# DVE, ACT and POOL choose their next operation by a due time that is found backward from TensorE's order, over rounds of planning

## The chip, the cores and the metric

The kernel runs on one core of a Trainium2 chip. The metric is the device time of one execution in microseconds (us), as a median over runs. One further execution is profiled, and every row below is from that one. The engines are called PE (TensorE matmul), PEld (TensorE weight load), DVE (VectorE), ACT (ScalarE), POOL (GpSimd) and SP, which issues nearly all DMAs.

## The reference

Random-feature attention for 8 batches of 8 heads (576 positions, head size 64, 128 features), then a gated MLP on the 4608 rows that come out of it (512 to 1536 and back).

```python
q_s, k_s = q * scale, k * scale
phi(x) = exp(h - max(h)) / sqrt(m),  h = x @ omega.T - sum(x*x)/2
kv  = einsum('bhsm,bhsd->bhmd', phi(k_s), v);  z = sum over s of phi(k_s)
num = einsum('bhsm,bhmd->bhsd', phi(q_s), kv)
den = einsum('bhsm,bhm->bhs', phi(q_s), z) + 1e-6
x   = (num / den) laid out as [4608, 512]
out = ((x @ w_a) * (x @ w_b)) @ w_out
```

## The kernel before

**Work.** Attention goes pair by pair of heads (32 pairs, four to a batch). The MLP goes in nine blocks of 512 rows: blocks 0 to 7 are the first 512 positions of each batch, block 8 is the last 64 positions of all eight batches. While the MLP of one batch runs, attention of the next fills in. fp32 operands of the MLP are split into a high and a low part (`hilo`, `split`, `convert`), and each product is three matmuls. Blocks 0 and 1 multiply plainly (`moe_block`, L1074) while ACT and DVE still convert the weights; blocks 2 to 8 use seven half-size products where eight would do plainly (`moe_block7`, `product`, L1165), and blocks 7 and 8 do so for the output projection too (`Out7`, L971; otherwise L903).

**What hangs on what.** In `moe_block7` the products of a unit share two PSUM tiles p0 and p1. After each pair DVE adds them into a tile c (L1175), and only then may PE write p0 or p1 again. At the end of two units DVE multiplies two c tiles (L1214), ACT or DVE casts the result to the high part of `ghl`, DVE subtracts for the low part (L283), and the output products read `ghl`. Outputs of blocks 0 to 6 are copied from PSUM to `osb` by ACT or DVE and stored by SP; `osb` has two places, raw0 and raw1, so a copy waits until the store from its place has landed. Block 8 gets its rows from DRAM: a DMA brings `xl`, ACT casts it to `x` (one cast for each quarter, x_0 to x_3).
The pair work has a burst on PE (L696 with L764 and L766): it needs `kl` and `hq`, which come back transposed by way of DRAM, and writes pkv and pm.

**Order.** Nothing here is in program order: the kernel first records a graph of 5661 operations, each with engines that may do it, a cost, and a priority number `prio` written by hand (adds into c -12, casts to ghl -10, output sums -7 to -9, weight conversion 4000 to 8000, attention 1000 times the pair, PE's MLP products 10**6 upward). `Graph.schedule` plans them one after another on modelled engines and rings of tiles, and the kernel issues each engine's instructions in the planned order. Among the operations that could start on an engine, the one with the lowest key is planned next:

```python
wait = CFG["WAIT"] if e == "DVE" and 0 <= o.prio < 4000 else 0
key = (max(s - wait, free[e] + 30), o.prio, o.n)
```

At run time each engine goes through its own list in that order, and each instruction waits for its semaphores. What the model has wrong turns into waits. An operation that lists two engines (casts to ghl, copies to osb, casts of weights) goes to the one that the plan finds earlier.

Of the kernel before, what the change touches and what calls it, by code (L numbers as in the profile page):

```python
# [35 lines left out]
EPS = 1e-6 * M  # L36
KS = NHP

CFG = dict(ZS=800, ZB=(1500, 3000, 5000), ZD=(1500, 3000, 4500), HQ=(2500, 4000, 5000), BACK2=(1500, 2500, 4000), TW=(), WAIT=150, RAW=2000, FAST=(0, 1, 2, 3), JOIN0=False, WARM=8, HROOM=["w0", "u1", "w1", "u2", "w2", "u3"], H=3, TURN=(7,), BACK=1500, AT=2, GATES=(-4, -1, 2, 5), SQPE=4, MARGIN=1200, LOAD=2500, SUMS=1000, NATS=(1, 2, 3), CONV=(28000, 2600))

# [8 lines left out]


class Op:
    __slots__ = ("eng", "fn", "deps", "prio", "alloc", "margin", "n", "end", "start", "after", "bytes", "need", "at")


class Graph:
# [15 lines left out]
    def op(self, eng, fn, r=(), w=(), prio=0, alloc=(), deps=(), margin=0, nbytes=0, at=0):  # L73

        o = Op()
        o.eng, o.fn, o.prio, o.alloc, o.margin, o.bytes = eng, fn, prio, list(alloc), margin, nbytes
        o.n, o.end, o.start, o.at = len(self.ops), None, None, at
        found = set(deps)
        for b in o.alloc:
            b.born = o  # L80
        found.update(b.born for b, _ in (*r, *w) if b.born is not None)
        for b, part in r:
            found.update(x for x, p in b.writers if p is None or part is None or p == part)
        for b, part in w:
            found.update(x for x, p in b.writers + b.readers if p is None or part is None or p == part)
        for b, part in w:
            keep = lambda l: [(x, p) for x, p in l if not (part is None or p == part)]
            b.writers, b.readers = keep(b.writers) + [(o, part)], keep(b.readers)
            b.users.append(o)
        for b, part in r:  # L90
            b.readers.append((o, part))
            b.users.append(o)
        for b in o.alloc:
            if b.ring in self.rings:
                self.rings[b.ring]["order"].append(b)
        found.discard(o)
        o.deps = list(found)
        self.ops.append(o)
        return o
# [13 lines left out]
    def place(self, o):  # L113
# [16 lines left out]
            got.append((b, best[1]))  # L130
        return t, got

    def schedule(self, bw=330.0, dma_lat=2000):
        engines = ("PE", "ACT", "DVE", "POOL", "SP")
        free = dict.fromkeys(engines, 0)
        dma_free = 0
# [20 lines left out]
        while len(done) < len(self.ops):  # L157
            best = None
            for e in engines:
                mine = None  # L160
                for o in ready[e]:
                    at = self.place(o) if o.alloc else (0, ())
                    if at is None:
                        continue
                    s = max(free[e], o.need, at[0])
                    for x in o.eng:
                        if x != e and max(free[x], o.need, at[0]) + o.eng[x] <= s + o.eng[e] - (o.eng[e] <= o.eng[x]):
                            break
                    else:


                        wait = CFG["WAIT"] if e == "DVE" and 0 <= o.prio < 4000 else 0
                        key = (max(s - wait, free[e] + 30), o.prio, o.n)
                        if mine is None or key < mine[0]:
                            mine = key, s, o, at[1]
                if mine and (best is None or mine[1] < best[1]):
                    best = (*mine, e)
# [57 lines left out]
def tile_attention_moe(ctx: ExitStack, tc: tile.TileContext, kqt, kqtt, kqn, kqnt, vx, omst, idn, wab, wout, out):  # L235
# [1045 lines left out]

    order = g.schedule()
    with tc.manual_schedule():
        for o in order:
            for b in o.alloc:
# [70 lines left out]
```

## Time and profile before

| what | value |
|---|---|
| median of 3 runs | 1063.78 us (1063.69 to 1069.8) |
| the profiled execution | 1066.55 us, its span 1064.7 us |
| mean granted TensorE clock | 0.998 |
| busy share: DVE, ACT, POOL | 84%, 56%, 10% |
| DMA | 314.16 MB, mean 295 GB/s |

The span is the time from the first to the last instruction; 1.85 us of the profiled execution lie around it. The profiled execution is 2.77 us above the median. A matmul's recorded end is modelled and overlaps the next matmul, so what PE loses at a place is best read from start to start.

### The profile page before, as it was taken

What the parts mean: (1) busy time and instruction counts of PE and PEld (TensorE: products, weight loads), DVE (VectorE), ACT (ScalarE), POOL (GpSimd) and SP (SyncE); (2) the same over time, 40 slices, a digit from 0 to 9 for tenths busy, and PEclk for the clock granted to TensorE, in tenths of its full rate; (3) what the DMA queues carried; (4) which work ended last, traced back from release to release, by engine and by line L of the source; (5) the groups of instructions that cost most, each with busy time, mean ns of one, the idle gap of its engine ahead of it and who ended that gap; (6) DMA issues with size and microseconds to landing.
All of it is one profiled execution on the core that took longest, in us unless ns stands there. A gap on an engine that the chain in (4) does not pass through costs nothing.

```text
span 1064.7 us, 22028 instructions
## 1 busy us (share of the span) xinstructions
PE 1045.8 (98%) x7806; PEld 920.4 (86%) x7806; DVE 892.0 (84%) x2233; ACT 599.1 (56%) x1646; POOL 107.5 (10%) x177
## 2 busy tenths in 40 slices
PE   9999999999989999999999999999999999999997
PEld 7877777777779888888888888888889988999997
DVE  6999998899997788778878889778777768998766
ACT  7999787667575574657455665666563233233211
POOL 0111111111111010111011111111010000000000
PEclk9999999999999999999999999999999999999999
DMA  9867878999899889999899888988888798899981
GB/s 357 304 228 243 278 260 282 300 345 311 284 309 359 275 285 302 335 312 289 308 328 311 299 303 296 336 293 272 270 294 275 257 336 286 306 335 342 349 304 45
DMA packets 123614, 314.16 MB, mean 295 GB/s; under 512 B 17648, under 2 KB 40944, under 8 KB 123504
## 3 DMA queue, kind: packets, MB, share of 16 engines
q1 hardware_dynamic: 122640, 312.10, 86.3%
q8 instruction: 61, 1.00, 0.4%
q10 hardware_dynamic: 864, 0.66, 0.2%
q14 instruction: 49, 0.40, 0.1%
HBM read 255.52 MB, written 57.18 MB: 294 GB/s over the span
## 4 chain that ended last, share of the span: by engine, by line
PE 77%; DVE 13%; DMA 4%; ACT 3%; issue 2%; SPq 0%; ACTq 0%; DVEq 0%
PE p L1165 37%; PE o L903 18%; PE ppk L454 5%; PE o_P L971 4%; PE pa L1074 3%; PE pb L1074 2%; PE pkv L696 2%; PE pm L764 2%; DVE zero L715 1%; DVE c L1175 1%; DVE sm L477 1%; DMA td<-ts 1%; DMA out_dram<-osb 1%; PE pn L838 1%; DVE ghl L283 1%
## 5 line engine op out<-in xcount | busy, mean ns | idle before, releaser
L1175 DVE TENSOR_TENSOR c<-p,c 128x512 f32<-128x512 f32 (+1 forms) x336 | 207.9, 619 | 92.5 <-PE p L1165 89.9
L903 PE MATMUL o<-wo,ghl 128*128 128x512 f32 x1008 | 270.1, 397 | 0.8 <-DVE ghl L283 0.8
L903 PEld LDWEIGHTS o<-wo,ghl 128*128 128x128 f32 x1008 | 176.1, 188 | 33.4 <-DVE ghl L283 1.6
L1165 PE MATMUL p<-Sa,t 128*128 128x256 f32 x1008 | 141.4, 281 | 0.0
L1165 PEld LDWEIGHTS p<-Sa,t 128*128 128x128 f32 x1008 | 131.0, 188 | 4.4
L649 POOL TENSOR_TENSOR z<-hk 128x256 f32<-128x256 f32 x56 | 43.9, 783 | 660.3 <-ACT hk L490 559.5
L275 ACT COPY c<-p 128x256 f32<-128x256 f32 x84 | 31.1, 370 | 120.3 <-PE p L1165 66.8
L725 ACT ACTIVATE hq<-hq,dn 128x128 f32<-128x128 f32 x224 | 71.0, 393 | 39.4 <-DVE dn L721 39.4
L454 PEld LDWEIGHTS ppk<-om,X 64*128 64x128 f32 x504 | 61.8, 189 | 18.3 <-issue 5.2
L715 DVE CUSTOM_DVE_ANT_0 zero<-hq,zb 128x128 bf16<-128x128 f32 x224 | 75.0, 335 | 2.9 <-ACT c L275 0.2
L454 PE MATMUL ppk<-om,X 64*128 64x128 f32 x504 | 74.6, 288 | 2.3 <-ACT k L275 2.1
L1165 PE MATMUL p<-x,t 128*128 128x256 f32 x504 | 74.4, 284 | 0.8 <-ACT oc L275 0.8
L1165 PE MATMUL p<-Sb,t 128*128 128x256 f32 x504 | 74.6, 284 | 0.0
L1074 PE MATMUL pa<-x,wa 128*128 128x512 f32 x288 | 73.8, 399 | 0.5 <-ACT a L275 0.5
L1074 PE MATMUL pb<-x,wb 128*128 128x512 f32 x288 | 73.0, 398 | 1.2 <-ACT xts L275 0.6
L1165 PEld LDWEIGHTS p<-x,t 128*128 128x128 f32 x504 | 69.3, 190 | 5.5 <-ACT oc L275 1.0
L454 PE MATMUL ppq<-om,X 64*128 64x128 f32 x504 | 73.0, 286 | 0.6 <-ACT hq L275 0.3
L1165 PE MATMUL p<-Sb,bq 128*128 128x256 f32 x504 | 73.6, 282 | 0.0
L1165 PE MATMUL p<-x,wb 128*128 128x256 f32 x504 | 70.1, 283 | 2.5 <-DVE c L1175 2.4
L490 ACT ACTIVATE hk<-hk,sm 128x128 f32<-128x128 f32 x184 | 59.3, 393 | 23.0 <-DVE sm L485 22.9
L1165 PEld LDWEIGHTS p<-x,wb 128*128 128x128 f32 x504 | 65.7, 188 | 6.2 <-DVE c L1175 3.1
L1165 PE MATMUL p<-x,wa 128*128 128x256 f32 x504 | 69.9, 284 | 1.0 <-DVE c L1175 1.0
(192 smaller groups left out, 2025.6 us busy)
## 6 DMA issues: line engine op xcount, KB each, us to landing
t<-td SPq DMA_DIRECT2D x168, 512.0 KB
wo<-wod SPq DMA_DIRECT2D x96, 512.0 KB
bq<-bd SPq DMA_DIRECT2D x84, 256.0 KB
qdr<-qd SPq DMA_DIRECT2D x112, 160.0 KB
hq<-qdr SPq DMA_DIRECT2D x28, 640.0 KB
X<-in_kqt_dram SPq DMA_DIRECT2D x30, 512.0 KB
raw<-in_wab_dram SPq DMA_DIRECT2D x24, 512.0 KB
td<-ts SPq DMA_DIRECT2D x24, 512.0 KB
```

The costliest lines, as they stand in the source:

```text
L275: nc.scalar.copy(o(), i())
L454: nc.tensor.matmul(pps[w].ap[:, c * M:c * M + M], x()[rows, c * P:c * P + P], om.ap[rows], start=True, stop=True)
L490: g.op({"ACT": 392}, lambda e, c=c, w=w, to=to, at=at: nc.scalar.activation(to.ap[:, at + c], src[w](c), AF.Exp, scale=SC, bias=sm.ap[:, 2 ...
L649: g.op({"POOL": pool2(n)}, lambda e: nc.gpsimd.tensor_tensor(o(), a(), c(), op=ALU.add), r=r, w=w, alloc=list(al), prio=pri, deps=zload[-1 ...
L696: nc.tensor.matmul(pkv.ap[D * j:D * j + D, 0:M], vb.ap[:, vc, 0:D], c(), start=(n == 0), stop=(n == 4))
L715: g.op({"DVE": 413}, lambda e, c=c, j=j, rr=rr, qc=qc: nc.vector.tensor_tensor_reduce(out=junk.ap[rr], in0=qc(), in1=zb.ap[rr, j], scale=1 ...
L725: g.op({"ACT": 392}, lambda e, c=c, src=src: nc.scalar.activation(hq.ap[:, c], src(), AF.Copy, scale=dn.ap[:, c:c + 1]), r=[sd, (dn, None) ...
L903: nc.tensor.matmul(po.ap[:], ghl.ap[:, gi, t * P:(t + 1) * P], wo.ap[:, wi], start=(n == 0 and i == 0), stop=(n == NF - 1 and i == 2))
L971: nc.tensor.matmul(pb.ap[:, t], A[0](ai)[:, t * P:(t + 1) * P], W[0](wi), start=begin and t == j == 0, stop=stop and t == 1 and j == 2)
L1074: nc.tensor.matmul(pb.ap[:], wt.ap[:, wi, c], xs[c].at(xi), start=(c == 0 and i == 0), stop=(c == NC4 - 1 and i == 2))
L1165: nc.tensor.matmul(pb.ap[:, half], wcol(wi, c), xc(xi, c), start=n == 0, stop=n == 5)
L1175: g.op({"DVE": dve(n)}, lambda e: nc.vector.tensor_tensor(c4.ap[:, o], pb.ap[:, half], y(), op=ALU.add), r=[*((pb, k) for k in range(half. ...
```

## The change

`Graph.plan` takes the place of the one call of `schedule`. It plans once as before. Then, three times, `dues` goes backward through the last plan: each PE operation is due when that plan had it, less all idle time of PE up to it, and every other operation is due at the least of its users' due times less their cost and latency; the next plan uses the due time instead of `prio` among DVE's, ACT's and POOL's candidates. PE and SP still choose by `prio`. Of the four plans the one with the earliest planned end is issued. No operation is added or taken out and no cost is changed; the graph has the same dependencies.

```diff
-CFG = dict(ZS=800, ...
+CFG = dict(EDF=("DVE", "ACT", "POOL"), ROUNDS=3, SQUEEZE=1, ZS=800, ...
...
+    def dues(self):
...
+        last = {}
+        for o in self.order:
+            for b in o.alloc:
+                if b.slot in last:
+                    for x in last[b.slot].users:
+                        if x is not o:
+                            after[x].append(o)
+                last[b.slot] = b
+        idle, at, ideal = 0, 0, {}
+        for o in self.order:
+            if "PE" in o.eng:
+                idle += max(0, o.start - at - 5) * CFG["SQUEEZE"]
+                at = o.end
+                ideal[o] = o.start - idle
+        for o in reversed(self.order):
+            d = ideal[o] + o.eng["PE"] if o in ideal else inf
+            for n in after[o]:
+                same = "PE" in o.eng and "PE" in n.eng
+                cost = n.end - n.start if n.bytes else next(iter(n.eng.values()))
+                d = min(d, n.due - cost - n.margin - (0 if same else self.LAT + (150 if "PE" in o.eng else 0)))
+            o.due = d
+
+    def plan(self):
+
+        self.schedule()
+        plans = [(max(o.end for o in self.order), 0, None)]
+        for k in range(CFG["ROUNDS"]):
+            self.dues()
+            due = {o: o.due for o in self.ops}
+            self.schedule()
+            plans.append((max(o.end for o in self.order), k + 1, due))
+        _, k, due = min(plans, key=lambda p: p[:2])
+        if k < CFG["ROUNDS"]:
+            for o in self.ops:
+                o.due = due and due[o]
+            self.schedule()
+        return self.order
...
-                        key = (max(s - wait, free[e] + 30), o.prio, o.n)
+                        pr = o.prio if o.due is None or e not in CFG["EDF"] else o.due
+                        key = (max(s - wait, free[e] + 30), pr, o.n)
...
-    order = g.schedule()
+    order = g.plan()
```

The order moves nearly everywhere. Both programs issue the same instructions on PE, POOL and SP; 37 operations go from ACT to DVE and 23 from DVE to ACT (31 of the 60 are casts to ghl, 11 copies to osb). Copies to osb on DVE become 9 where there were 4. Three places follow. Line numbers of the changed kernel are 54 higher.

**ACT in block 7, around the third cast of xl.** `c_11` is the product of two c tiles, `ghl_3` and `ghl_2` its high parts, which PE needs for its next output product; `x_3<-xl` is for block 8. Before:

```order
L275 CAST x_2_11235<-xl_10950 128x512
L275 CAST ot_01_11262<-otf_10928 128x2x256
L275 COPY c_20_11296<-p_3770 128x256
L275 CAST x_3_11314<-xl_11265 128x512
L275 CAST ghl_3_11324<-c_11_11213 128x512
L275 CAST ghl_2_11333<-c_11_11213 128x256
L275 CAST og_10_11363<-ogf_10_11351 128x256
```

The same place now:

```order
L329 CAST ot_01_11245<-otf_10973 128x2x256
L329 COPY c_20_11320<-p_3782 128x256
L329 CAST ghl_3_11330<-c_11_11213 128x512
L329 CAST ghl_2_11340<-c_11_11213 128x256
L329 CAST ot_10_11343<-otf_11278 128x2x256
L329 CAST x_3_11352<-xl_11275 128x512
L329 CAST ot_11_11375<-otf_11278 128x2x256
L329 CAST og_10_11378<-ogf_10_11370 128x256
```

The cast of xl has moved behind both casts to ghl.

**PE and DVE where block 2 begins.** `p_3770` and `p_3771` are p0 and p1 (now `p_3782` and `p_3783`), `bq` and `t` weights. PE before:

```order
L1165 MATMUL p_3770<-Sb_0_3435,t_001_2694 128x256 x3
L1165 MATMUL p_3770<-Sb_1_3713,t_001_2694 128x256 x3
L1165 MATMUL p_3771<-x_2_3289,t_001_2694 128x256 x3
L1165 MATMUL p_3771<-x_3_3583,t_001_2694 128x256 x3
L1165 MATMUL p_3771<-Sb_0_3435,bq_00_3781 128x256 x3
L1165 MATMUL p_3771<-Sb_1_3713,bq_00_3781 128x256 x3
L1165 MATMUL p_3770<-x_0_2633,wb_724 128x256 x3
L1165 MATMUL p_3770<-x_1_2973,wb_724 128x256 x3
L1165 MATMUL p_3771<-x_2_3289,wb_724 128x256 x3
```

PE there now:

```order
L1219 MATMUL p_3782<-Sb_0_3389,t_001_2724 128x256 x3
L1219 MATMUL p_3782<-Sb_1_3742,t_001_2724 128x256 x3
L750 MATMUL pkv_2_3887<-hk_2_3683,v_1_3306 64x128 x8
L750 MATMUL pkv_2_3887<-htk_3077,v_1_3306 64x128 x2
L818 MATMUL pm_0_3889<-hq_0_3340,kl_3870 64x512 x2
L820 MATMUL pkv_2_3887<-hq_0_3340,kl_3870 64x64 x2
L1219 MATMUL p_3783<-x_2_3267,t_001_2724 128x256 x3
L1219 MATMUL p_3783<-x_3_3525,t_001_2724 128x256 x3
L1219 MATMUL p_3783<-Sb_0_3389,bq_00_3796 128x256 x3
L1219 MATMUL p_3783<-Sb_1_3742,bq_00_3796 128x256 x3
L1219 MATMUL p_3782<-x_0_2625,wb_704 128x256 x3
L1219 MATMUL p_3782<-x_1_2941,wb_704 128x256 x3
```

The pair's burst now stands between the product into p0 and the next use of p0; before it came after the whole unit. DVE before:

```order
L283 TENSOR_TENSOR ts_3854<-tf_3789,ts_3854 128x2x256
L1175 TENSOR_TENSOR c_00_3793<-p_3770,c_00_3793 128x512
L665 STREAM_TRANSPOSE z_3_2_3751<-zs_2_3752 128x256
L666 TENSOR_REDUCE zq_2_3887<-z_3_2_3751 128x8
L1175 TENSOR_TENSOR c_00_3793<-p_3770,c_00_3793 128x256
L715 ISA zero,dn_1_3837<-hq_1_3666,zb_1_3652 128x128
L715 ISA dn_1_3837 128x1
L1175 TENSOR_TENSOR c_00_3793<-p_3771,c_00_3793 128x512
```

DVE there now, from the end of the pair's divisors on:

```order
L774 TENSOR_SCALAR dn_1_3829<-dn_1_3829 128x9
L775 RECIPROCAL dn_1_3829<-dn_1_3829 128x9
L337 TENSOR_TENSOR x_0_3890<-pm_0_3889,x_0_3890 128x256
L331 COPY osb_2_3936<-o_2_2521 128x512
L1229 TENSOR_TENSOR c_00_3809<-p_3783,c_00_3809 128x512
L331 COPY osb_3_3953<-o_3_2532 128x512
L1229 TENSOR_TENSOR c_01_3961<-p_3783,c_01_3961 128x2x256
```

Two copies to osb, which ACT did before, stand in front of two adds into c.

**PE at the end of the program.** `ghl_11` is the last high and low part, `o_P` the sums of the output, `og` and `ot` the operands of output products. Before:

```order
L1165 MATMUL p_3771<-x_2_11235,t_511_13053 128x256 x3
L1165 MATMUL p_3771<-x_3_11314,t_511_13053 128x256 x3
L1165 MATMUL p_3771<-Sb_0_12118,bq_51_13075 128x256 x3
L1165 MATMUL p_3771<-Sb_1_12123,bq_51_13075 128x256 x3
L971 MATMUL o_P_12516<-ot_41_12903,og_42_13141 128x256 x6
L971 MATMUL o_P_12560<-wo_9_12759,og_43_13144 128x256 x6
L971 MATMUL o_P_12393<-wo_11_12944,ghl_11_13251 128x256 x6
```

Now:

```order
L1219 MATMUL p_3783<-Sb_0_12112,bq_51_13075 128x256 x3
L1219 MATMUL p_3783<-Sb_1_12117,bq_51_13075 128x256 x3
L1025 MATMUL o_P_12418<-ot_40_12877,og_40_13114 128x256 x6
L1025 MATMUL o_P_12460<-ot_40_12877,og_41_13117 128x256 x6
L1025 MATMUL o_P_12516<-ot_41_12903,og_42_13157 128x256 x6
L1025 MATMUL o_P_12558<-wo_9_12761,og_43_13167 128x256 x6
L1025 MATMUL o_P_12393<-wo_11_12946,ghl_11_13245 128x256 x6
```

Four output products stand between the last product of the unit and the first that reads ghl_11, where two stood.

## Rows read from the trace of the kernel before

**Rows 1.** The page: busy us (share of span) xinstructions.

```profile
PE 1045.8 (98%) x7806; PEld 920.4 (86%) x7806; DVE 892.0 (84%) x2233; ACT 599.1 (56%) x1646; POOL 107.5 (10%) x177
```

**Rows 2.** Windows: length, busy us (x) of PE, PEld, DVE, ACT, POOL, clock, DMA share.

```profile
900.00:950.00 50.00, 48.32 (x395) 48.08 (x394) 47.47 (x103) 15.92 (x35) 0.00 (x0) 0.97 0.89 306
```

**Rows 3.** Timeline of PE, 899 to 907: start, us, instructions [idle before, releaser].

```profile
900.24 0.87 PE L1165 MATMUL p<-Sa,t 128*128 128x256 f32 x6
902.79 1.03 PE L971 MATMUL p<-wo,ghl 128*128 128x256 f32 x6 [1.68 <-issue]
...
904.78 1.48 PE L971 MATMUL o_P<-wo,og 128*128 128x256 f32 x6
```

**Rows 4.** Timeline of ACT, the same stretch.

```profile
900.22 0.62 ACT L275 CAST x<-xl 128x512 fp32r<-128x512 f32 x1 [3.13 <-DMA xl<-xtd]
900.75 0.92 ACT L275 CAST ghl<-c 128x512 fp32r<-128x512 f32 x2
```

**Rows 5.** Timeline of DVE, the same stretch.

```profile
898.40 1.28 DVE L1214 TENSOR_TENSOR c<-c,c 128x512 f32<-128x512 f32 x2
...
901.39 0.69 DVE L283 TENSOR_TENSOR ghl<-c,ghl 128x512 fp32r<-128x512 f32 x1 [1.37 <-ACT ghl L275]
...
902.60 0.42 DVE L283 TENSOR_TENSOR ghl<-c,ghl 128x256 fp32r<-128x256 f32 x1
```

**Rows 6.** Timeline of SP's queue: the DMA that this cast waits for.

```profile
894.37 0.32 SPq L286 DMA_DIRECT2D xl<-xtd  x1
```

**Rows 7.** Windows of 2 us after it, columns as in rows 2.

```profile
904.00:906.00 2.00, 2.00 (x11) 2.00 (x11) 1.95 (x6) 1.00 (x3) 0.00 (x0) 0.50 0.77 197
906.00:908.00 2.00, 2.00 (x14) 2.00 (x13) 1.38 (x5) 0.41 (x1) 0.00 (x0) 0.68 0.66 195
```

**Rows 8.** Timeline of PE where block 2 begins.

```profile
310.06 0.88 PE L1165 MATMUL p<-Sb,bq 128*128 128x256 f32 x6
312.01 0.98 PE L1165 MATMUL p<-x,wb 128*128 128x256 f32 x6 [1.07 <-DVE c L1175]
314.32 0.97 PE L1165 MATMUL p<-x,wb 128*128 128x256 f32 x6 [1.33 <-DVE c L1175]
```

**Rows 9.** Timeline of DVE there.

```profile
310.66 0.69 DVE L283 TENSOR_TENSOR ts<-tf,ts 128x512 fp32r<-128x512 f32 x1
311.27 0.69 DVE L1175 TENSOR_TENSOR c<-p,c 128x512 f32<-128x512 f32 x1
...
313.58 0.69 DVE L1175 TENSOR_TENSOR c<-p,c 128x512 f32<-128x512 f32 x1
```

**Rows 10.** Timeline of PE: the pair's burst after that unit.

```profile
318.77 1.09 PE L696 MATMUL pkv<-hk,v 128*64 128x128 f32 x16
...
320.99 1.21 PE L1165 MATMUL p<-x,wa 128*128 128x256 f32 x8
```

**Rows 11.** Timeline of all engines, the end of the program.

```profile
1050.26 0.87 PE L1165 MATMUL p<-Sb,bq 128*128 128x256 f32 x6
...
1050.98 0.87 PE L971 MATMUL o_P<-ot,og 128*128 128x256 f32 x6
...
1051.69 0.87 PE L971 MATMUL o_P<-wo,og 128*128 128x256 f32 x6
...
1053.35 0.50 PE L971 MATMUL o_P<-wo,ghl 128*128 128x256 f32 x2 [0.79 <-ACT ghl L275]
...
1054.31 4.26 PE L971 MATMUL o_P<-wo,ghl 128*128 128x256 f32 x34 [0.46 <-DVE ghl L283]
...
1060.01 0.69 DVE L976 TENSOR_TENSOR oc<-p,oc 128x512 f32<-128x512 f32 x1 [0.71 <-PE p L971]
```

**Rows 12.** Timeline of PE in block 0: one of the scattered gaps.

```profile
90.40 1.88 PE L1074 MATMUL pb<-x,wb 128*128 128x512 f32 x7 [0.51 <-DVE wb L283]
```

**Rows 13.** Waits: who waited for whom, us in total, times, longest us.

```profile
ACT osb L275 <- DMA out_dram<-osb: 12.2, 11, 3.2
```

**Rows 14.** Timeline of PE at the start.

```profile
0.99 3.59 PE L304 MATMUL none<-zero 128*128 128x512 bf16 x8 [0.99 <-DVE zero L297]
```

More of the change, by code (lines that the diff above doesn't have):

```diff
@@ L37 @@
 KS = NHP
-CFG = dict(ZS=800, ZB=(1500, 3000, 5000), ZD=(1500, 3000, 4500), HQ=(2500, 4000, 5000), BACK2=(1500, 2500, 4000), TW=(), WAIT=150, RAW=2000, FAST=(0, 1, 2, 3), JOIN0=False, WARM=8, HROOM=["w0", "u1", "w1", "u2", "w2", "u3"], H=3, TURN=(7,), BACK=1500, AT=2, GATES=(-4, -1, 2, 5), SQPE=4, MARGIN=1200, LOAD=2500, SUMS=1000, NATS=(1, 2, 3), CONV=(28000, 2600))
+CFG = dict(EDF=("DVE", "ACT", "POOL"), ROUNDS=3, SQUEEZE=1, ZS=800, ZB=(1500, 3000, 5000), ZD=(1500, 3000, 4500), HQ=(2500, 4000, 5000), BACK2=(1500, 2500, 4000), TW=(), WAIT=150, RAW=2000, FAST=(0, 1, 2, 3), JOIN0=False, WARM=8, HROOM=["w0", "u1", "w1", "u2", "w2", "u3"], H=3, TURN=(7,), BACK=1500, AT=2, GATES=(-4, -1, 2, 5), SQPE=4, MARGIN=1200, LOAD=2500, SUMS=1000, NATS=(1, 2, 3), CONV=(28000, 2600))
 class Buf:
@@ L53 @@
 class Op:
-    __slots__ = ("eng", "fn", "deps", "prio", "alloc", "margin", "n", "end", "start", "after", "bytes", "need", "at")
+    __slots__ = ("eng", "any", "due", "fn", "deps", "prio", "alloc", "margin", "n", "end", "start", "after", "bytes", "need", "at")
 class Graph:
@@ L75, in op @@
         o = Op()
+        o.any, o.due = eng, None
         o.eng, o.fn, o.prio, o.alloc, o.margin, o.bytes = eng, fn, prio, list(alloc), margin, nbytes
@@ L131, in place @@
         return t, got
-    def schedule(self, bw=330.0, dma_lat=2000):
+    def dues(self):
+        inf = 1e12
+        after = {o: [(n, o) for n in ()] for o in self.ops}
+        for o in self.ops:
+            for d in o.deps:
+                after[d].append(o)
+        last = {}
[29 more added lines that the diff above has]
+        if k < CFG["ROUNDS"]:
+            for o in self.ops:
+                o.due = due and due[o]
+            self.schedule()
+        return self.order
+    def schedule(self, bw=330.0, dma_lat=2000):
+        for r in self.rings.values():
+            r["at"] = 0
+        for s in self.slots:
+            self.slots[s] = None
+        for o in self.ops:
+            o.eng, o.start, o.end = o.any, None, None
         engines = ("PE", "ACT", "DVE", "POOL", "SP")
```

## The prediction

> **What bounds the kernel now.** I read the page first. PE is busy for 1045.8 of 1064.7 us [rows 1], DVE for 892.0, ACT for 599.1: PE sets the end, and the change leaves PE's work as it is. So the question is what PE loses. The rest of the span is 1064.7 - 1045.8 = 18.9 us. Of it 1.0 lies before the first matmul [rows 14] and 1064.7 - 1060.0 = 4.7 after the last, from the last add on [rows 11]. No order of DVE or ACT touches the first; the second is an add and a store, the same in both kernels. That leaves 13.2 us inside the program. Even all of it would be 1.2%.
>
> Then I looked where it lies, from start to start. A product of six matmuls takes PE 0.71 us when nothing waits (1050.98 to 1051.69, rows 11). Three places stand out.
>
> X, block 7: the product of 900.24 is followed at 902.79, 2.55 us later, so 1.84 are lost [rows 3]. ACT shows why: at 900.22 it casts xl after 3.13 us of idling for the DMA, and the two casts to ghl come behind it [rows 4], although DVE had the c tiles done at 898.40 + 1.28 = 899.68 and then itself idles 1.37 us for ghl [rows 5]. The DMA was issued at 894.37 [rows 6] and so took 5.85 us to be usable. [...]
>
> B, where block 2 begins: 310.06 to 312.01 and 312.01 to 314.32, that is 1.95 and 2.31 us for 0.71 each, 2.84 lost [rows 8]. PE waits for the adds into c; DVE was busy with work of the weight sums (L283) and of the pair right in front of them [rows 9].
>
> T, the tail: 1051.69 to 1053.35, and two matmuls that last until 1054.31: (1.66 - 0.71) + (0.96 - 0.24) = 1.67 lost, waiting for ghl [rows 11].
>
> The idle times of these places are 1.68, 1.07 + 1.33 and 0.79 + 0.46, together 5.3 us [rows 3, 8, 11]. So 13.2 - 5.3 = 7.9 us are scattered in gaps of some tenths, such as the 0.51 us wait for a weight conversion in block 0 [rows 12].
>
> **The change part by part.** No instruction is added, so each term is a gap that closes or opens.
>
> T. Four output products now cover the chain from the last product to ghl_11 where two did. The chain itself is unchanged, on DVE and ACT alike, so the two further products take 2 x 0.71 = 1.42 us out of the loss and 0.25 stay. They are taken from earlier places in the same block, where PE had them as filler; a gap that opens there belongs to N below. I take 1.4; the bounds are 0 and 1.67.
>
> X. The cast of xl now stands behind both casts to ghl, so PE's next output product no longer hangs on that DMA. This gives back 1.84 us and, as the clock then has no reason to fall, half of 2.00 us and 0.32 of 2.00 us [rows 7], 1.64: together 3.5. The lower bound is 0: the cast still waits for the DMA, and now a cast to ot and those to og stand behind it. Their users come some products later, so I take 3.5.
>
> B. The pair's burst moves between the product into p0 and the next use of p0. It lasts 320.99 - 318.77 = 2.22 us [rows 10], more than the 1.24 us that were lost first. That loss is covered. For the second add PE has one product, 0.71 us, and needs the add's 0.69 plus the 0.17 by which a product's end lies behind its successor's start [rows 8, 9]: 0.15 us stay. So 2.84 - 0.15 = 2.7. The lower bound is 0: the burst now runs about 9 us earlier (318.77 against 310.06 - 0.71) and needs hq back from DRAM, which before was not asked of it at that point.
>
> S and N. Of the 7.9 scattered us some close (S) and, as nearly all of DVE's and ACT's order is new, others open (N). Casts and subtractions for weights, x and og stand earlier against PE than they did; adds into c and the subtractions for ghl, on which most products wait, have the same one or two products of cover as before, since the dependencies fix that. S lies between 0 and 7.9. N is not in any row; its nearest rows are the same gaps, so it lies between 0 and 7.9 too. I set them equal, 4 each, and they cancel.
>
> The copies to osb. DVE has nine, five more than before. What is queued behind them on DVE is an add into c, and PE waits for that. A copy waits until the store from its place has landed; ACT waited for this 11 times, 12.2 us in all, 3.2 at most [rows 13], and there it cost PE little. I cost it at nothing beyond N, since the mean is 1.1 us and five of the nine write a place that was last stored from a block earlier; without that cover it is the first rival.
> [...] The row at 900.22 shows a copy that waits for a DMA and holds the ready casts behind it for over a microsecond [rows 4]. [...]
>
> Sum: 1.4 + 3.5 + 2.7 = 7.6 us. From the profiled execution that is 1066.55 - 7.6 = 1059.0. The profiled execution is 2.8 us above the median. If that is X, a DMA's landing that another execution may not have, the median has only T and B to give: 1063.78 - 4.1 = 1059.7. Both ways I come to 1059, which is 0.45% less.
>
> **The rivals.**
> First, DVE behind a store (slower). Price of one: 3.2 us of waiting less the 0.71 of one product, 2.5, and 1.64 for the clock if it falls as after X: 4.1. Three of them make 1059 + 12.4 = 1071. It is slower than before from 1063.8 - 1059 = 4.8 us on, so from the second. For it: the order puts two such copies between adds at the start of block 2. Against it: the mean wait is a third of the longest, and none of the five waits of PE in rows 3, 8 and 11 was for a copy to osb. Chance 0.12.
> Second, new gaps for old: N is 7.6 us larger than S, and the end stays at 1064. For it: a plan from modelled costs can be tight only where the model is right, and due times leave less in hand on purpose. Chance 0.20.
> Third, the scattered gaps go as well: S = 7.9 and N = 0 give 1059 - 7.9 = 1051. For it: weights, x and og come earlier nearly everywhere. Against: the adds into c have no more cover than before. Chance 0.15.
> Fourth, X only moves, to the casts of ot and og behind the cast of xl: 1059 + 3.5 = 1062.5. Chance 0.10.
> That the change does not do what it says is out: the issued order differs from the first plan's at all three places, so a replanned order was kept.
>
> **How the numbers follow.** My forecast has what is left, 0.43, and lies at 1059 with about 3 us to either side. The range is 1051 to 1067: the third rival is its lower end (S = 7.9, N = 0), and N = 7.9 with S = 0 the upper, 1059 + 7.9. Outside lie the first rival and the edge of the third, under 0.2. A change of 1%, about the least that a measurement of this kernel tells from none, is 10.6 us: faster means below 1053.1, slower above 1074.4. Below 1053.1 lies most of the third rival and a little of the forecast, 0.13; above 1074.4 the worse half of the first, 0.06; 0.81 stays within.
>
> **What would show it.** In the profile after, PE's start to start at the first output product of ghl_2 in block 7 should be 0.7 to 0.9 us, and no stretch should have a granted clock below 1.00. At the start of block 2, PE should run the burst and four products with no wait over 0.3 us. At the end two matmuls should wait about 0.25 us for ghl. PE's idle time should fall from 18.9 to about 14 us. DVE idling for stores of osb by more than 1 us a time, with PE idle behind it, would show the first rival; PE idle still near 18.9 in other places the second; near 10 the third. The prediction is wrong if the burst of block 2 waits for hq, or if a cast or copy that waits for a DMA now heads DVE's queue.

## The result and the profile after

The change makes the kernel slower by 0.27%: 1068.66 us (median of 22 runs) against 1065.65 us for the kernel before beside it, ratio 1.0027, 95% interval 1.0019 to 1.0035. The profiled execution of the changed kernel took 1067.19 us, 1.5 us below its median.

Two of the three large gaps of before went as forecast, the third mostly moved, and others opened or grew ahead of it. The page of the changed kernel, engine by engine as in [rows 1]:

```profile
PE 1046.6 (98%) x7806; PEld 922.1 (87%) x7806; DVE 898.4 (84%) x2247; ACT 590.4 (55%) x1632; POOL 107.5 (10%) x177
```

PE's idle time is 1065.4 - 1046.6 = 18.8 us, as before (18.9). DVE has 14 instructions more and ACT 14 less than in [rows 1]: work that both may do has gone from ACT to DVE. The windows of the changed kernel (length, busy us of PE, PEld, DVE, ACT, POOL, granted clock, DMA share, GB/s):

```profile
30.00:160.00 130.00, 127.62 (x810) 100.68 (x810) 127.59 (x325) 108.74 (x284) 21.23 (x30) 1.00 0.79 265
150.00:200.00 50.00, 47.00 (x273) 36.78 (x273) 43.13 (x125) 37.51 (x104) 8.48 (x14) 0.97 0.83 281
300.00:350.00 50.00, 48.18 (x350) 42.93 (x351) 42.43 (x117) 28.47 (x80) 6.66 (x12) 0.97 0.95 343
900.00:950.00 50.00, 49.99 (x421) 49.66 (x420) 49.70 (x108) 14.88 (x34) 0.00 (x0) 1.00 0.92 314
...
184.00:186.00 2.00, 1.53 (x12) 1.45 (x14) 1.82 (x2) 1.25 (x5) 0.00 (x0) 0.66 1.01 404
186.00:188.00 2.00, 2.00 (x11) 1.58 (x10) 1.64 (x5) 1.07 (x2) 0.00 (x0) 0.50 1.07 397
300.00:302.00 2.00, 2.00 (x16) 1.68 (x17) 1.93 (x5) 1.12 (x3) 0.00 (x0) 0.67 0.92 324
302.00:304.00 2.00, 2.00 (x6) 1.52 (x6) 1.97 (x7) 1.87 (x4) 0.00 (x0) 0.50 1.00 383
```

The stretch of block 7 that had 48.32 us of PE and a mean clock of 0.97 [rows 2] now has 49.99 and 1.00. Two other stretches have taken its place at 0.97, with the clock at 0.50 for a while in each. DVE is busy for 127.6 of the 130 us from 30 to 160.

PE's timeline in the changed kernel (start, us, instructions [idle before, releaser]), in the order of the program:

```profile
52.62 0.73 PE L1128 MATMUL pa<-x,wa 128*128 128x512 f32 x2 [1.28 <-DVE x L337]
...
184.47 0.67 PE L508 MATMUL ppk<-om,X 64*128 64x128 f32 x2 [2.73 <-ACT k L329]
...
299.41 0.49 PE L508 MATMUL ppk<-om,X 64*128 64x128 f32 x2 [1.80 <-ACT hk L329]
...
313.88 1.09 PE L750 MATMUL pkv<-hk,v 128*64 128x128 f32 x16
...
317.62 0.87 PE L1219 MATMUL p<-x,wb 128*128 128x256 f32 x6
319.07 0.98 PE L1219 MATMUL p<-x,wb 128*128 128x256 f32 x6 [0.58 <-DVE c L1229]
...
323.46 0.98 PE L1219 MATMUL p<-x,wa 128*128 128x256 f32 x6
325.69 0.98 PE L1219 MATMUL p<-x,wa 128*128 128x256 f32 x6 [1.24 <-DVE c L1229]
...
905.40 0.87 PE L1219 MATMUL p<-Sa,t 128*128 128x256 f32 x6
906.11 0.87 PE L1025 MATMUL p<-wo,ghl 128*128 128x256 f32 x6
...
1053.65 0.87 PE L1025 MATMUL o_P<-wo,og 128*128 128x256 f32 x6
1054.35 4.77 PE L1025 MATMUL o_P<-wo,ghl 128*128 128x256 f32 x36
...
1054.86 4.07 PEld L1025 LDWEIGHTS o_P<-wo,ghl 128*128 128x128 f32 x34 [0.31 <-DVE ghl L337]
```

From the end: at 1054.35 the last products follow after 0.70 us where two waits stood [rows 11]. At 906.11 the output product that waited for `xl`'s cast follows after 0.71 us, where before it took 2.55 [rows 3]. At the start of block 2 the burst does stand ahead of the second add (313.88), but two waits have opened instead: 1.45 - 0.71 = 0.74 us lost at 319.07 and 2.23 - 0.71 = 1.52 at 325.69. Ahead of that stand three waits that before had not, or had smaller: 1.28 us at 52.62, 2.73 at 184.47 (1.40 before) and 1.80 at 299.41 (0.33 before). PE's timeline of before at the last two places:

```profile
182.94 0.48 PE L454 MATMUL ppk<-om,X 64*128 64x128 f32 x2 [1.40 <-ACT k L275]
...
298.39 0.37 PE L454 MATMUL ppq<-om,X 64*128 64x128 f32 x1 [0.33 <-ACT hq L275]
```

What PE waited for there. First ACT's timeline of the changed kernel:

```profile
181.24 2.44 ACT L779 ACTIVATE hq<-hq,dn 128x128 f32<-128x128 f32 x8 [0.75 <-DVE dn L775]
...
184.16 0.26 ACT L329 COPY k<-pkv 128x128 f32<-128x128 f32 x1
...
297.58 1.29 ACT L329 CAST ts<-tf 128x512 fp32r<-128x512 f32 x2 [1.24 <-DVE tf L1165]
298.78 0.58 ACT L329 COPY hk<-ppk 128x512 f32<-128x512 f32 x1
```

Both times ACT's list has work at its head that waits for DVE (0.75 us for dn, 1.24 for tf), and the copy that frees PE's PSUM tile stands behind it. At 184 the larger part is ACT's own work: eight scalings of hq, 2.44 us, stand ahead of the copy of k. ACT's timeline of before at that place has three of them there; the other five come behind the copy:

```profile
181.15 0.98 ACT L725 ACTIVATE hq<-hq,dn 128x128 f32<-128x128 f32 x3
...
182.61 0.28 ACT L275 COPY k<-pkv 128x128 f32<-128x128 f32 x1
```

The five make 2.44 - 0.98 = 1.46 us, about what the wait has grown by (2.73 - 1.40 = 1.33). Then DVE's timeline of the changed kernel:

```profile
50.90 0.94 DVE L337 TENSOR_TENSOR wb<-raw,wb 128x512 fp32r<-128x512 f32 x1
51.87 0.69 DVE L337 TENSOR_TENSOR x<-px,x 128x512 fp32r<-128x512 f32 x1
...
317.73 0.69 DVE L331 COPY osb<-o 128x512 f32<-128x512 f32 x1 [0.31 <-DMA out_dram<-osb]
318.33 0.68 DVE L1229 TENSOR_TENSOR c<-p,c 128x512 f32<-128x512 f32 x1
...
324.49 1.15 DVE L1229 TENSOR_TENSOR c<-p,c 128x256 f32<-128x256 f32 x2 [0.86 <-PE p L1219]
```

At 50.90 us DVE still converts weights, and the low part of x, for which PE waits, comes behind. At 317.73 an osb copy stands ahead of the add into c. At 324.49 DVE is not late: it idles 0.86 us for PE's product, and PE then waits for the two adds behind it. At 298 ACT took the copy of hk in the order of its list: it idled 1.24 us until 297.58 for the casts of ts and made the copy behind them, at 298.78, although PE had finished the tile that the copy reads by about 296 us (its last matmul by 295.74 + 0.27 = 296.01).

### The profile page after: what moved, and what is told of

The parts are those of the page before. It is cut to its first block, busy times and chain, and to the rows that moved or that the text cites. A ratio compares the mean times of both kernels' runs of the same rounds, so it can differ in the third digit from the quotient of the medians.

```text
span 1065.4 us, 22048 instructions
## 1 busy us (share of the span) xinstructions
PE 1046.6 (98%) x7806; PEld 922.1 (87%) x7806; DVE 898.4 (84%) x2247; ACT 590.4 (55%) x1632; POOL 107.5 (10%) x177
## 4 chain that ended last, share of the span: by engine, by line
PE 70%; DVE 19%; DMA 5%; ACT 3%; issue 2%; SPq 0%; ACTq 0%; DVEq 0%
PE p L1219 37%; PE o L957 15%; PE o_P L1025 4%; PE ppk L508 4%; DVE zero L769 2%; DMA out_dram<-osb 2%; PE pkv L750 2%; DVE sm L531 2%; DVE raw L383 2%; PE pm L818 1%; DVE ghl L337 1%; DVE sq L495 1%; DVE a L1136 1%; DVE tf L1165 1%; PE p L1025 1%
## 5 line engine op out<-in xcount | busy, mean ns | idle before, releaser
L1219 PE MATMUL p<-Sa,t 128*128 128x256 f32 x1008 | 144.0, 281 | 0.0
L544 ACT ACTIVATE hq<-hq,sm 128x128 f32<-128x128 f32 x192 | 64.0, 395 | 20.6 <-DVE sm L539 20.5
L1128 PE MATMUL pb<-x,wb 128*128 128x512 f32 x288 | 75.2, 404 | 0.0
L1219 PEld LDWEIGHTS p<-x,wa 128*128 128x128 f32 x504 | 65.2, 188 | 5.6 <-DVE c L1229 2.7
```

The lines of the kernel that those rows point to most:

```text
L544: g.op({"ACT": 392}, lambda e, c=c, w=w, to=to, at=at: nc.scalar.activation(to.ap[:, at + c], src[w](c), AF.Exp, scale=SC, bias=sm.ap[:, 2 ...
L1128: nc.tensor.matmul(pb.ap[:], wt.ap[:, wi, c], xs[c].at(xi), start=(c == 0 and i == 0), stop=(c == NC4 - 1 and i == 2))
L1219: nc.tensor.matmul(pb.ap[:, half], wcol(wi, c), xc(xi, c), start=n == 0, stop=n == 5)
```

## The experiments

To place the losses I use one measure for all kernels, worked out from the traces: for each group of matmuls, its start on the chip less the sum of the planner's own TensorE costs for all groups ahead of it. How much this lateness grows over a stretch is what PE lost there, clock included, whatever the order. Each kernel has one trace, so each row is one execution. The stretches are from 25 to 340 us of planned TensorE time ("start"), 340 to 850 ("middle") and 850 to the end. Kernels that share a start by construction agree within 0.9 us there (before 12.3, late340 11.8, late850 12.2; convert_act 10.0, splice 10.9). "Shared" counts, in the plan, the instructions that DVE or ACT may do and that DVE has in the first 200 us.

| kernel | due times order | shared on DVE | start | middle | end | ratio to before (95%) |
|---|---|---|---|---|---|---|
| before | none | 36 | 12.3 | -0.3 | 6.3 | 1 |
| nudge_before | none | 38 | 15.6 | 1.3 | 4.1 | 1.0029 (1.0017 to 1.0040) |
| nudge2_before | none | 37 | 11.2 | 2.3 | 4.6 | 1.0012 (1.0002 to 1.0023) |
| late340 | all, from 340 us | 36 | 11.8 | 2.2 | 1.2 | 0.9989 (0.9977 to 1.0001) |
| late850 | all, from 850 us | 36 | 12.2 | -0.4 | 1.5 | 0.9964 (0.9950 to 0.9977) |
| changed kernel | all | 43 | 17.6 | 1.2 | 1.2 | 1.0027 (1.0019 to 1.0035) |
| nudge_after | all | 40 | 16.8 | 3.3 | 3.8 | 1.0039 (1.0025 to 1.0054) |
| nudge2_after | all | 43 | 16.1 | 1.9 | 1.7 | 1.0020 (1.0011 to 1.0028) |
| early340 | all, up to 340 us | 43 | 17.2 | 0.2 | 4.2 | 1.0051 (1.0037 to 1.0065) |
| pin4 | all | 43 | 17.1 | 1.4 | 1.2 | 1.0018 (1.0010 to 1.0027) |
| osb_act | all | 40 | 16.8 | 2.2 | 2.7 | 1.0038 (1.0024 to 1.0052) |
| act_only | ACT | 41 | 13.7 | 1.9 | 5.8 | 1.0027 (1.0017 to 1.0038) |
| dve_only | DVE | 32 | 9.9 | 0.4 | 1.3 | 0.9947 (0.9935 to 0.9960) |
| nudge_dve | DVE | 29 | 12.2 | 1.6 | 4.2 | 1.0011 (1.0002 to 1.0021) |
| nudge2_dve | DVE | 29 | 9.9 | 5.3 | 1.3 | 0.9947 (0.9933 to 0.9961) |
| convert_act | all | 10 | 10.0 | 2.9 | 6.2 | 1.0011 (1.0002 to 1.0020) |
| convert_act_nudge | all | 12 | 8.8 | 1.8 | 4.3 | 0.9972 (0.9961 to 0.9984) |
| splice | all, not 340 to 850 us | 10 | 10.9 | 1.3 | 1.5 | 0.9970 (0.9959 to 0.9981) |
| share19 | all | 27 | 7.0 | 2.2 | 2.6 | 0.9939 (0.9925 to 0.9953) |
| share19_nudge | all | 31 | 10.7 | 2.0 | 1.2 | 0.9958 (0.9943 to 0.9973) |

Part of what sets the rule's starts apart are falls of the granted clock (2 us windows show 0.50 in the changed kernel and pin4, 0.53 in nudge_before), 1.7 us each by the clock alone: in that stretch the changed kernel and pin4 have two, nudge_after one of double length (a mean of 0.91 from 160 to 190 us, where the changed kernel has 0.94), early340 (0.94 there), nudge2_after and osb_act (0.99 each from 160 to 312), act_only (0.98 from 190 to 270) and nudge_before one, the others none. With these taken off whole, the four starts with all three engines by due times and nothing else changed are 13.4 to 15.5, and the five by priority 11.2 to 13.9.

**Theories.** The first: the changed order loses at the start and gains at the end, stretch by stretch. The rival: any new order deals the gaps out anew, wherever plan and chip differ. A third: the copies to osb on DVE.

**Splitting by time: late340, early340, late850.** The due times of the round that the change keeps are used in a part of the plan only; the other part goes by priority as before.

```diff
-                        pr = o.prio if o.due is None or e not in CFG["EDF"] else o.due
+                        pr = o.due if o.due is not None and e in CFG["EDF"] and ("MASK" not in CFG or free[e] >= 340000) else o.prio
...
-        if k < CFG["ROUNDS"]:
-            for o in self.ops:
-                o.due = due and due[o]
-            self.schedule()
+        for o in self.ops:
+            o.due = due[o]
+        CFG["MASK"] = True
+        self.schedule()
```

(early340 has `free[e] < 340000`, late850 `free[e] >= 850000`.) Expected of late340:

> The order by due times is used only from 340 us of the plan on; up to there each engine's order is that of the kernel before. If the loss sits at the start (blocks 0 and 1, attention and weight conversion together), the gaps at 52.6, 184.5, 299.4 and 325.7 us and the two falls of the granted clock behind them are gone and the gains behind 850 us stay: 1065.7 less 1.4 (tail) less 3.5 (block 7) = about 1061, ratio to before 0.994 to 0.997. If any new order only deals the gaps out anew, the part from 340 to 850 us brings as many new ones as the end saves: ratio 0.999 to 1.002. If the copies of the output on VectorE cost by waiting for their stores, most of them lie behind 340 us, and the time stays above before: 1.001 to 1.003.

Of early340:

> The mirror image: order by due times up to 340 us of the plan, by priority behind it. If the loss sits at the start, this keeps all of it and gives up the gains behind 850 us: 1068.7 plus 3 to 5 = 1071 to 1074, ratio to before 1.005 to 1.008, and the gaps of 52.6, 184.5, 299.4 and 319 to 326 us stand in it as in the changed kernel. If gaps are only dealt out anew, it lies where the changed kernel lies or below, 1.000 to 1.003.

Of late850:

> Due times only from 850 us of the plan on, where the prediction put its two largest gains: the tail and the cast of xl in block 7; everything ahead is as in before, instruction for instruction. If both gains are real and stand alone: 1.4 + 3.5 = 4.9 us less, about 1060.5, ratio 0.994 to 0.997. If a gap taken away there returns within the stretch, 0.998 to 1.000.

late340 came out at -0.11% with an interval that touches no change, early340 at +0.51%: the loss is the first part's, and the two halves add up (+0.40%) to about the +0.27% of the whole. late340 gained less than I had said: its middle loses 2.2 us. That need not be the rule, since a kernel by priority (nudge2_before, below) loses 2.3 there. late850, with nothing but the last part, gains 0.36%, 3.8 us (2.5 to 5.3), where the prediction's T and X add to 4.9. PE's timeline of late850 at the place of X:

```profile
898.59 0.87 PE L1219 MATMUL p<-Sa,t 128*128 128x256 f32 x6
899.30 0.87 PE L1025 MATMUL p<-wo,ghl 128*128 128x256 f32 x6
```

and its window there:

```profile
900.00:950.00 50.00, 49.68 (x418) 49.29 (x417) 49.31 (x109) 15.52 (x36) 0.00 (x0) 1.00 0.92 323
```

0.71 us and a clock of 1.00: the gain of X stands by itself.

early340 also shows that losses at the start do not simply add up, since up to there its order is that of the changed kernel. PE's timeline of early340 at the start of block 2, then DVE's:

```profile
316.43 0.87 PE L1219 MATMUL p<-x,wb 128*128 128x256 f32 x6
319.06 0.98 PE L1219 MATMUL p<-x,wb 128*128 128x256 f32 x6 [1.75 <-DVE c L1229]
```

```profile
317.71 0.69 DVE L331 COPY osb<-o 128x512 f32<-128x512 f32 x1 [0.73 <-DMA out_dram<-osb]
```

In early340 the clock did not fall behind the wait at 299 (1.00 from 300 to 304), and PE comes to this place 317.62 - 316.43 = 1.19 us earlier than in the changed kernel. Yet the second product starts at 319.06 in one and at 319.07 in the other: in both, the osb copy ahead of DVE's add waits for its store, until 317.71 and 317.73. What the second fall of the clock cost in the changed kernel was lost here anyway, to the first rival.

**Moving four places by hand: pin4.** The rows that stand ahead of the late ones at 49, 184, 298 and 317 us are moved behind them, in the list that is issued.

```diff
     order = g.plan()
+    for to, ns in CFG["PIN"]:
+        moved = [o for o in order if o.n in ns]
+        order = [o for o in order if o.n not in ns]
+        k = next(i for i, o in enumerate(order) if o.n == to) + 1
+        order[k:k] = moved
```

> The changed kernel with four places of its order moved by hand: five of the scalings of hq of block 2, pair 0, behind the x cast and the k2 copy (ScalarE, 184 us), the two ts casts behind the hk and hq copies (ScalarE, 298 us), three weight conversions behind the low part of x_0_3 (VectorE, 49 us), one output copy behind the add into c (VectorE, 317 us). If these rows ahead of them are the cause, the gaps go from 2.8 to 1.3, 1.97 to 0.2, 1.55 to 0.2 and 0.74 to 0.1 us and the two clock falls with them (1.6 us each): 5.0 + 3.2 = about 8 us less, 1060 to 1062, ratio to before 0.994 to 0.997. If the waits only move on to the next late piece, under 2 us of it is seen: 1.001 to 1.003.

It gave 1.4 us of the 8 by the medians, and the intervals of the two kernels overlap. The waits at 52.62, 299.41 and 319.07 are gone, and the one at 184 split into two without a fall of the clock. But others opened; PE's timeline of pin4:

```profile
54.55 1.87 PE L1128 MATMUL pa<-x,wa 128*128 128x512 f32 x5 [1.90 <-ACT a L329]
...
306.68 0.98 PE L1219 MATMUL p<-x,wa 128*128 128x256 f32 x6 [1.91 <-DVE a L1136]
```

DVE's timeline of pin4 ahead of the last of them:

```profile
305.94 0.69 DVE L1136 TENSOR_TENSOR a<-pb,a 128x512 f32<-128x512 f32 x1
```

DVE has no idle time there and comes to the multiply by `a` at 305.94, in the changed kernel at 306.10. With the wait at 299 taken away, PE only arrives earlier at a DVE that is as late as ever. So at this place the order of ACT's rows, which I had blamed, does not set the time. It suggests a cause that none of the three theories had: the start is short of DVE.

**One engine at a time: dve_only, act_only.** As above, with the condition `e == "DVE"` or `e == "ACT"`.

> Due times order VectorE alone, ScalarE and GpSimd keep the order by priority. If the loss is ScalarE's (k2 and hk copies behind scalings and casts), the gaps at 184 and 299 us are gone and the time falls below before: ratio 0.994 to 0.998. If it is VectorE's (output copies and conversions ahead of what TensorE waits for), the loss stays: 1.001 to 1.005. If gaps are dealt out anew, anything from 0.997 to 1.003, with the gaps in other places than either kernel has them.

> Due times order ScalarE alone; VectorE and GpSimd keep the order by priority. If the rule harms on ScalarE and helps on VectorE, and the two add up, this is the changed kernel less what VectorE gave: +2.9 + 6.2 = about 9 us above before, 1.006 to 1.010. If only the two together harm, it lies near before, 0.998 to 1.002.

dve_only is 0.53% faster than before, act_only 0.27% slower. That looks as if the rule helped on DVE and harmed on ACT; but the two do not add up as expected (act_only has no 0.6 to 1.0%), and the next runs show how far one plan can be trusted.

**Is it chance? The nudges.** One constant of the planner's model is changed by 1 to 2.5%, no rule.

```diff
-    def schedule(self, bw=330.0, dma_lat=2000):
+    def schedule(self, bw=330.0, dma_lat=2050):
```

(1980 in the second ones; the variants with due times keep one round of planning, the round that the changed kernel uses.)

> The kernel before, ordered by priority, with one constant of the planner's model, the latency that it assumes for a transfer, 2050 instead of 2000 ns; no rule is changed, but many instructions come in another order. If the rule of order makes the time, this stays at before, ratio 0.999 to 1.001. If the gaps are dealt out by chance, by where the plan and the chip differ, it is off by as much as the whole change was: below 0.998 or above 1.002.

> The changed kernel (its first round of planning, which is the one it uses) with the same 2050 ns. If the rule makes the time, it stays at 1.002 to 1.004 of before, with gaps at about the places of the changed kernel. If the gaps are dealt out by chance, it comes out elsewhere, between 0.995 and 1.006, with the gaps in other places.

> Due times on VectorE alone, as in dve_only (0.9947), with the same 2050 ns. If what helps is the rule on VectorE, this too is at 0.993 to 0.997. If dve_only was a lucky deal, this lies anywhere from 0.995 to 1.005, its middle at 1.000.

> The kernel before with the planner's latency of a transfer at 1980 ns. If the rule makes the time: 0.999 to 1.001. If chance deals: its distance from before is as large as that of the first nudge (0.3%) as often as not, to either side.

> The changed kernel (its one round of planning) with 1980 ns. If the order by due times costs by itself: 1.002 to 1.004, as its two sisters had 1.0027 and 1.0039. If chance deals: anywhere from 0.995 to 1.005.

> Due times on VectorE alone with 1980 ns. If the rule on VectorE helps by itself: below 0.998. If dve_only (0.9947) was the lucky one and its nudge (1.0011) the common one: 0.998 to 1.003.

The kernel before, nudged, is 0.29% and 0.12% off; dve_only goes from 0.9947 to 1.0011 and back to 0.9947. So a single comparison of two plans of this kernel leaves 0.3 to 0.6% open, and +0.27% alone would prove nothing of the rule. But chance does not seem to be all: by stretch, every start with due times on all three engines and nothing else changed loses 16.1 to 17.6 us (four traces, three plans), every one by priority 11.2 to 15.6, every one with DVE alone 9.9 to 12.2. (For the falls of the clock in these numbers see above.)

**The third theory: osb_act.** Copies to osb only on ACT.

```diff
+    for o in g.ops:
+        if o.any.keys() == {"ACT", "DVE"} and o.prio == -5:
+            o.any = {"ACT": o.any["ACT"]}
     order = g.plan()
```

> The changed kernel (its one round of planning), but the output copies run on ScalarE alone, none on VectorE behind a store. If those copies were the loss (the first rival), the time goes back to before or below: 0.995 to 1.000. If they were not, it stays where the changed kernel is, 1.001 to 1.005.

+0.38%, and a start of 16.8: the osb copies are not what makes the start long, though one of them does hold PE up at 319.07.

**DVE's load: convert_act, convert_act_nudge, splice.** The same edit with `o.prio > -10`: all shared work but the casts to ghl on ACT.

> The changed kernel (its one round of planning), but the instructions that may run on ScalarE or VectorE, apart from the casts to ghl, run on ScalarE alone: the conversions of weights, the output copies, qT (39 of the 73 that VectorE has in the changed kernel). If the loss is VectorE's load at the start (busy 127.6 of 130 us from 30 to 160 us, where before has 125.9), that load falls by about 13 us up to 340 us of the plan, the gaps at 52.6, 184.5 and 299.4 us go, and the time falls below both: 1058 to 1063, ratio 0.993 to 0.998. If the gaps are dealt out by chance whatever VectorE's load, it lies anywhere from 0.996 to 1.005.

> As convert_act, with the planner's latency of a transfer at 2050 instead of 2000 ns. If VectorE's load is the cause, it stays within 2 us of convert_act, below before: 0.993 to 0.998. If chance deals, it lies anywhere from 0.996 to 1.005 and 3 us or more from convert_act is as likely as not.

The splice is convert_act with the order by priority from 340 to 850 us of the plan.

> Up to 340 us of the plan the order of convert_act (conversions and output copies on ScalarE, due times), from 340 to 850 us the order by priority, from 850 us on due times as in the changed kernel. If each stretch keeps its own gaps: convert_act ends the first product of block 3 at 415.9 us, before takes 448.2 us from there to the first outputs of block 6, the changed kernel 180.2 us from there to its last matmul, in sum 1044.3 us where before has 1055.0: about 10 us less, with 1.2 us of idle that this plan shows at 751 us about 9, ratio 0.990 to 0.993. If a stretch's gaps come anew when its surroundings change, it lies anywhere from 0.995 to 1.003.

The start falls to 10.0, 8.8 and 10.9 with the rule on all three engines, 5 to 9 us less than with the free choice. Behind 340 us these plans lose some of it again, so convert_act ends 0.11% above before and its nudge 0.28% below, 4.4 us apart where I had expected 2 at most. The window of convert_act, as in the changed kernel's first one:

```profile
30.00:160.00 130.00, 126.32 (x821) 100.65 (x821) 119.67 (x307) 122.86 (x316) 21.77 (x30) 1.00 0.78 263
```

DVE is down by 7.9 us here, ACT up by 14.1. The splice missed its sum (9 us) and gave 0.30%: its middle and end cost what the borrowed plans had cost within 1.6 us, but I had read convert_act's first stretch at a point (416 us) where the splice already had other orders.

**Fewer shared instructions on DVE: share19, share19_nudge.** All three engines by due times, free choice, but 19 shared instructions that the changed kernel has on DVE and dve_only on ACT (ten conversions of weights, seven casts to ghl in block 0, one qT and one osb copy) may run on ACT only.

```diff
+    for o in g.ops:
+        if o.n in CFG["ONACT"]:
+            o.any = {"ACT": o.any["ACT"]}
     order = g.plan()
```

> The changed kernel (its one round of planning), with 19 of the shared instructions of the first 200 us of the plan, which it has on VectorE and dve_only on ScalarE, allowed on ScalarE only; all three engines by due times. If VectorE's load is what costs at the start, the loss from 25 to 340 us of TensorE's work falls from 16.1 to 17.5 us to 9 to 13, and the time below before: 1058 to 1063, ratio 0.993 to 0.998. If ScalarE's order by due times costs by itself, the loss stays at 15 to 17 and the time at 1.000 to 1.004.

> As share19, with the planner's latency of a transfer at 1980 instead of 2000 ns. If VectorE's load is the cause: the loss at the start 9 to 13 us again, ratio 0.993 to 0.999 (what chance does behind 340 us comes on top, up to 5 us in the runs so far). If not: 15 to 17 us, 1.000 to 1.005.

0.9939 and 0.9958: the fastest kernel of the study, 1060.67 us against 1066.82 for before beside it, and its nudge close behind. Their starts are 7.0 and 10.7. The window of share19 from 30 to 160 us:

```profile
30.00:160.00 130.00, 128.36 (x810) 101.40 (x810) 126.05 (x316) 118.49 (x305) 20.78 (x30) 1.00 0.79 268
```

DVE is nearly as full as ever there; what has changed is what fills it. Windows from 30 us up to the add that lets PE write the second product of block 2 on `wb`, for before, the changed kernel and share19:

```profile
30.00:313.58 283.58, 277.25 (x1690) 219.00 (x1688) 267.12 (x697) 220.90 (x586) 47.02 (x66) 1.00 0.84 283
```

```profile
30.00:318.33 288.33, 280.97 (x1708) 221.51 (x1707) 272.65 (x716) 219.76 (x588) 46.24 (x66) 0.99 0.83 284
```

```profile
30.00:307.19 277.19, 274.12 (x1675) 216.54 (x1673) 263.62 (x681) 225.07 (x593) 45.16 (x66) 1.00 0.86 288
```

From 30 us on, DVE has 272.65 us of work ahead of this add in the changed kernel, 267.12 before and 263.62 in share19, and little else: it idles 15.7, 16.5 and 13.6 us. Not all of the 5.5 us between the first two are shared work: the changed kernel has the pair's burst, and what DVE does for it, ahead of this add. The groups by line of the changed kernel, 30 to 160 us, price a shared instruction on DVE (count | busy us, mean ns | idle before):

```profile
L331 DVE CAST wb<-raw 128x512 fp32r<-128x512 f32 x12 | 5.3, 438 | 0.0
...
L331 DVE CAST wo<-raw 128x512 fp32r<-128x512 f32 x6 | 3.3, 552 | 0.0
L331 DVE CAST wa<-raw 128x512 fp32r<-128x512 f32 x6 | 2.8, 465 | 0.0
```

24 of them take 11.4 us, 0.475 each. The changed kernel has 43 - 36 = 7 more than before: 3.3 us of a full engine, and its start lost 5.3 more. share19 has 16 less than the changed kernel, 7.6 us, and its start lost 10.6 less; share19_nudge has 12 less than nudge2_after, which plans with the same 1980 ns, 5.7 us, and lost 5.4 less. ACT had 130 - 108.7 = 21 us free in that window. The sizes go together, but the falls of the clock are in them, two in the changed kernel and none in share19.

The load is not all that differs. ACT's timeline of share19 at the place where the changed kernel waits 2.73 us:

```profile
179.87 0.28 ACT L329 COPY k<-pkv 128x128 f32<-128x128 f32 x1
...
183.20 2.45 ACT L779 ACTIVATE hq<-hq,dn 128x128 f32<-128x128 f32 x8
```

Here the copy stands ahead of all eight scalings, and PE waits 0.18 us for it. The changed kernel, its two nudges, early340 and osb_act all have the eight ahead of the copy and wait 2.06 to 2.74 us. So this wait went with another order of ACT, which the plan found when 19 instructions were bound to ACT. No run changes the engines and keeps the order, and none binds the 19 to ACT and keeps the order by priority.

## Why the prediction was wrong

The forecast of 1059 was 10 us too low, the range ended at 1067, and the sign was wrong; what happened is the second rival, new gaps for old, and somewhat more of it. The prediction took 1% for the least that can be told from no change; the interval here is 0.08% to either side. The 2.8 us by which the profiled execution of before lay above the median of three runs are 0.9 with 22 runs, so they need no X as their reason.

T was right: 0.25 of 1.67 us was to stay, and what is left is 0.31 that PE's weight loads wait. X was right in mechanism: 0.71 us from start to start and a clock of 1.00 from 904 to 908, where the 1.64 us of the forecast came from 0.50 and 0.68 [rows 7]; by late850 T and X together are worth 3.8 us (2.5 to 5.3), forecast 4.9. The fourth rival, that X only moves, is out.

B was sized wrongly. Of 2.84 lost, 0.15 was to stay; the first gap is gone, but 0.74 and 1.52 stand behind it, 2.26 in all. The burst did cover its add and did not wait for hq. The 0.74 are the osb copy ahead of the add. The 1.52 are lost at the product on `wa` in front of which the burst had stood [rows 10]: where it was taken away, PE has nothing to do while DVE makes the two adds. I had costed what the burst covers at its new place and nothing for the old one.

**The step that failed is "I set them equal, 4 each, and they cancel".** N was not the mirror of S. The places of the profile add up so: the wait at 52.62 is new, 1.28 us; that of 184.47 went from 1.40 to 2.73, that of 299.41 from 0.33 to 1.80; and the two falls of the clock cost 2 x (0.34 + 0.50) = 1.68 and 2 x (0.33 + 0.50) = 1.66 us. That is 1.28 + 1.33 + 1.47 + 3.34 = 7.4 us in three places, as much as T, X and B were to give. It is an upper bound: early340 has no second fall of the clock and is no earlier behind 319 us. I had argued that adds and subtractions keep their cover by the dependencies; the losers were others, the copies and the low part of attention that stand behind scalings and casts on ACT's list or conversions on DVE's.

Behind it lies a part of the change that I never costed: which engine does the shared work. I counted the osb copies (nine for four) and not the weight conversions; 14 instructions in all went to DVE. And I took DVE's share, 84% of the span, as room, where from 30 to 160 us the kernel before shows this:

```profile
30.00:160.00 130.00, 128.01 (x808) 101.73 (x807) 125.90 (x322) 111.54 (x294) 21.79 (x30) 1.00 0.78 259
```

That is 97% of DVE, so at the start DVE has as little room as PE. Most of the extra loss comes later, though: by the measure above the changed kernel lost 5.9 us from 25 to 150 us of planned time and 11.7 from there to 340, before 5.1 and 7.2, share19 4.3 and 2.7. Shown is that binding 19 shared instructions to ACT, with the rule left on all three engines, turns +0.27% into -0.61%, and that a nudged plan repeats it (-0.42%). Not shown is how much of this is DVE's load and how much the other order that the plan then finds, as at 184 us; nor whether the 19 would help the kernel before as much without the rule; nor why ACT's due times make the plan give DVE more of them. And how much of any plan's middle (-0.4 to 5.3 us) belongs to its rule stays open, since the nudges scatter as widely.

The first rival is out for the whole: one osb copy stands right ahead of a wait of PE, with 0.74 us lost at 319.07, and osb_act is no faster. At that place it did happen, as a copy at the head of DVE's queue that waits 0.31 us for its store, and 0.73 in early340. The prediction had named that as a sign of being wrong. The third, that the scattered gaps go too, was possible after all: in the stretch up to 340 us share19 lost 5.3 us less than before did.

## What to carry to other kernels

Read the busy shares by stage before asking what an order is worth: an engine at 84% of the span was at 97% from 30 to 160 us, and the shortest starts (7.0 and 8.8 us) belong to kernels with shared work kept off it. When a planner chooses both order and engine, count how many instructions change engine, and price them on the fuller one. Before a new rule is judged by one plan, change a constant of the model that should not matter: here that alone moved the time by 0.1 to 0.6%, as much as the rule or more.

## What was not expected of the hardware

Behind some single waits of PE the granted clock fell and raised their price, by some 1.7 us each: after 2.73 us of idling at 184.47 and after 1.80 at 299.41 it was 0.50 in one 2 us stretch of the windows and 0.66 or 0.67 in the one ahead. Before's two waits of 1.07 and 1.33 us at the start of block 2 [rows 8] had none of it (1.00 from 310 to 318). In pin4 the wait at 184 was broken into two by a short piece of matmul work (PE was busy for 1.05 of the 2 us from 184 to 186), and the clock of that stretch stayed at 1.00:

```profile
150.00:200.00 50.00, 48.20 (x287) 37.65 (x284) 43.99 (x124) 38.93 (x106) 8.10 (x14) 1.00 0.84 287
...
308.00:310.00 2.00, 2.00 (x8) 1.71 (x7) 2.00 (x6) 2.00 (x8) 0.81 (x2) 0.50 0.96 363
```

while behind its new wait of 1.91 us at 306.68 the clock fell as behind the others. The length of a wait alone does not tell which: behind early340's 1.75 us at 319.06 the clock stayed at 1.00, and in nudge_before it fell behind 1.33 us (and 0.58 us some 2 us earlier). PE's timeline of nudge_before, and its window behind it:

```profile
312.51 1.65 PE L1219 MATMUL p<-x,wb 128*128 128x256 f32 x6 [1.33 <-DVE c L1229]
```

```profile
314.00:316.00 2.00, 2.00 (x21) 1.92 (x22) 0.39 (x2) 0.98 (x3) 0.00 (x0) 0.53 1.02 401
```

Nor does a fall always cost in the end: the changed kernel, with the one at 300 us, and early340, without it, start the same product at 319.07 and 319.06.
